# Attention and two expert layers on one core: a new order for the attention round, and another queue for the first k

## Chip, cores and metric

One core of a Trainium2 chip. The metric is the device time in microseconds of one execution. The kernel before takes 916.21 us, the median of three runs (915.29 to 916.43).

## What is computed

Attention over 4 batches, 8 heads, 576 positions, head size 64, all in float32, mixed with a linear memory by a gate per head; then two dense layers. The two layers are not touched by the change.

```python
scores = scale * np.matmul(q, k.transpose(0, 1, 3, 2))      # causal mask follows
a = np.exp(scores - scores.max(-1, keepdims=True)); a /= a.sum(-1, keepdims=True) + 1e-09
local = np.matmul(a, v)
q_p = phi(q)                                                # phi(x) = max(x, 0) + min(exp(x), 1)
mem_out = einsum('bhsd,bhde->bhse', q_p, M_prev) / (einsum('bhsd,bhd->bhs', q_p, z_prev)[..., None] + 1e-06)
g = 1.0 / (1.0 + np.exp(-beta))[None, :, None, None]
attn = g * mem_out + (1 - g) * local
# then: x = _moe_ref(attn, w_in, w_out, g_ln); out = _moe2_ref(x, w_gate, w_val, w_out)
```

## The kernel before

Attention works on pairs of heads: 16 pairs (4 batches by 4 pairs of heads). The 576 positions of a head are four blocks of 128 and a tail of 64; the tails of both heads of a pair are one block more (block 4). What is done for one pair is cut into 77 steps. The string `ORDER` (line 21) lists the steps of one round of a loop, each with a distance: in round `it`, the step `s2_p:0` works on pair `it`, `tk_p:1` on the next pair, `x0_c:-2` on the pair two before. `run` (line 506) walks through the list once per round, from round -3 on, and leaves out pairs that don't exist. The whole of attention stands under `tc.manual_schedule()`, so each engine's queue has its instructions in just this order, and an engine waits at the first one that isn't ready. What follows attention is ordered by the framework.

The steps, by engine (a number is that of a block of queries, or for `t`, `a` and `g` of keys):

- TensorE: `tq_p`, `tk_p`, `tf_p` transpose q, k and the memory's queries (L265); `s0_p` to `s4_p` are the scores (L352, three passes of float32r); `g0_p`, `g1_p`, `t0_p` to `t3_p`, `tt_p`, `tc_p` transpose the weights (L398 to L432); the sums over keys are `x0_m`, `x1_m` (the memory's part, L444) and `a00`, `a01`, `a10` to `a14` (L459), which write the two halves of a PSUM tile's partitions, one head each. `x0_m`, `a01` and `a00` make the first 256 queries, `x1_m` and `a14` to `a10` the other 320.
- VectorE: `s*_m` adds the mask and takes maxima (L372); `n01_r`, `n23_r`, `n4_r` turn sums into factors (L384, L385); `ph_m` is the memory's phi (L306, L307); `tq_l`, `tk_l` the low parts of q and k (L284, L295); `ph_r` the memory's norm (L321 to L323); copies `g1_c`, `tc_c`, `x0_c`; and, for the layer that follows, a piece of its weights a round: `cv_a` (L108, L109), `cv_b` (L117, L122), `cv_l` (L504).
- ScalarE: the exponentials `s*_e` (L380) and `ph_e`, the high parts `tq_h`, `tk_h`, the other copies out of PSUM, and `cv_r`, `cv_h`.
- GpSimd: `n*_p` scales the weights (L389), `ph_g` and `ph_s` are the memory's products (L311, L328), `cv_p` (L496).
- SyncE issues the loads `lq`, `lk`, `lv`, `lz`, `cv_d`.

PSUM: the scores and the three transposes of a pair take turns on two tiles (tag `s`), the transposed weights on two (`t`), the sums on two (`x`). A step that takes a tile waits until the step that reads its last content is done. The tile `ex` of the weights' conversion is there once: `cv_a` of one piece overwrites what `cv_l` of the piece before has read.

In the order of before the sums of a pair stand in two places: `x0_m x1_m a13 a12 a11 a14 a10 a01` in one round, and `a00` after the scores `s3_p` in the next.

Of the kernel before, what the change touches and what calls it, by code (L numbers as in the profile page):

```python
# [18 lines left out]


ORDER = """
n23_r:-1 s1_e:0 s4_m:0 tt_c:-1 tc_c:-1 s3_m:0 lk:1 cv_r:-1 n3_p:-1 s0_e:0 s4_e:0 x1_c:-2 a00:-2 g1_p:-1 tf_p:0
t3_p:-1 g1_c:-1 tf_c:0 n2_p:-1 t3_c:-1 x0_c:-2 s2_p:0 t2_p:-1 t0_p:-1 cv_b:-1 ph_e:1 t2_c:-1 n4_r:0 n01_r:0 tq_p:1
cv_p:-1 n1_p:0 lz:1 t0_c:-1 t1_p:-1 g0_p:-1 cv_h:-1 tq_h:1 s2_m:0 t1_c:-1 ph_m:1 tk_p:1 tk_h:1 x0_m:-1 x1_m:-1
a13:-1 tq_l:1 tk_l:1 ph_g:1 n0_p:0 n4_p:0 cv_d:1 lv:0 a12:-1 a11:-1 a14:-1 a10:-1 ph_r:1 lq:2 ph_s:1 s3_e:0 s2_e:0
a01:-1 s1_p:1 s0_p:1 s1_m:1 tt_p:0 s0_m:1 g0_c:-1 tc_p:0 s4_p:1 cv_l:-1 s3_p:1 cv_a:0
""".split()


# [21 lines left out]
def kernel(  # L51
# [16 lines left out]
    nc = tc.nc  # L68
# [82 lines left out]
    class Attention:  # L151
# [69 lines left out]
            return self.ps.tile(shape, F32, tag=tag, name=name, bufs=2)  # L221


        def load_qk(self, n, t, src):
            b, hp = pairs[n]
            for hh in range(2):
                nc.sync.dma_start(
                    t[:, : 8 * D].rearrange("p (c h d) -> p c h d", h=2, d=D)[:, :, hh],
                    src[b, 2 * hp + hh, :S0, :].rearrange("(c p) d -> p c d", p=P),
                )  # L230
            nc.sync.dma_start(
                t[0:64, 8 * D : 10 * D].rearrange("p (h d) -> p h d", h=2),
                src[b, 2 * hp : 2 * hp + 2, S0:, :].rearrange("h p d -> p h d"),
            )
# [2 lines left out]
            self.load_qk(n, self.qt[n % 2], q)  # L237

        def lk(self, n, r):
            self.load_qk(n, self.kt[n % 2], k)  # L240

        def lv(self, n, r):
            b, hp = pairs[n]
# [608 lines left out]
```

## Time and profile before

| what | us |
|---|---|
| median of three runs | 916.21 |
| the profiled execution | 914.82 |
| its span, first to last instruction | 913.0 |
| TensorE busy in the span | 888.3 |
| one round of attention in its steady part | 13.29 |

The profile is of one execution. Its page gives busy shares over the whole span, in which attention is the first quarter; answers for a stretch of time show one round. A line of a timeline has the start, the duration, engine, line, operation, what is written and read, shapes, and in brackets how long the engine was idle before and what released it. Matmul durations are modelled at their ends, so the time that a matmul group takes is read from its start to the next one's.

### The profile page before, as it was taken

To read this page: it belongs to the slowest core of one execution; us is meant where nothing else is said; L and a number is where in the kernel's file an instruction comes from. 1 tells how busy PE (TensorE), PEld (TensorE's weight loads), DVE (VectorE), ACT (ScalarE), POOL (GpSimd) and SP (SyncE) were. 2 spreads that over 40 slices of the span, in tenths; PEclk is the share of its full clock that TensorE was granted. 3 is DMA by queue.
4 is the path that set the end of the run, shared out by engine and by line. 5 is a ranking of instruction groups with operands and counts; after the bars stand their busy time and mean duration, and the time that the engine had idled before them with its cause. 6 is when DMAs were issued, how large, how long until landed. Compare 5 with 4: busy or idle time off the path is not lost.

```text
span 913.0 us, 13960 instructions
## 1 busy us (share of the span) xinstructions
PE 888.3 (97%) x5224; PEld 753.2 (82%) x5224; DVE 567.2 (62%) x1321; ACT 432.1 (47%) x941; POOL 267.0 (29%) x322
## 2 busy tenths in 40 slices
PE   5899999999989999999999999999999999999998
PEld 4788788787778998999998888888888888888887
DVE  5899999999587655664825158366349735232324
ACT  3799999998577455464535333112122212111111
POOL 4566665666565211112400034021014103000000
PEclk9899999999999999999999999999999999999999
DMA  5243533443122100110300013012003200000113
GB/s 127 51 94 81 115 90 89 97 104 88 47 70 71 47 24 24 36 58 24 116 1 1 1 53 109 23 27 67 1 1 106 79 0 1 1 1 1 47 46 116
DMA packets 76291, 48.62 MB, mean 53 GB/s; under 512 B 62656, under 2 KB 62656, under 8 KB 76224
## 3 DMA queue, kind: packets, MB, share of 16 engines
q1 hardware_dynamic: 76224, 47.74, 19.1%
q8 instruction: 41, 0.67, 0.3%
q14 instruction: 26, 0.21, 0.1%
HBM read 43.00 MB, written 4.72 MB: 52 GB/s over the span
## 4 chain that ended last, share of the span: by engine, by line
PE 87%; DVE 7%; POOL 2%; ACT 1%; issue 1%; DMA 1%; SPq 1%; DVEq 0%; POOLq 0%; ACTq 0%
PE gv L730 32%; PE po L749 16%; PE po L648 9%; PE sc L352 8%; PE h L597 7%; PE x L459 5%; PE x L444 2%; PE pl L636 1%; PE trq L265 1%; DVE p L372 1%; PE trk L265 1%; PE trf L265 1%; DVE exwo L109 1%; DVE exwo L108 0%; DVE exwo L119 0%
## 5 line engine op out<-in xcount | busy, mean ns | idle before, releaser
L736 DVE TENSOR_TENSOR sg<-sg,gv 128x512 f32<-128x512 f32 (+1 forms) x60 | 38.0, 633 | 176.5 <-ACT sg L735 176.5
L735 ACT ACTIVATE sg<-gv 128x512 f32<-128x512 f32 (+1 forms) x60 | 33.1, 552 | 233.7 <-PE gv L730 233.7
L730 PE MATMUL gv<-xx,gh 128*128 128x512 f32 (+1 forms) x480 | 136.2, 368 | 0.2 <-ACT xx L138 0.2
L730 PE MATMUL gv<-xx,vh 128*128 128x512 f32 (+1 forms) x480 | 136.1, 368 | 0.0
L648 PE MATMUL po<-lnT,woh 128*128 128x256 f32 x576 | 104.9, 284 | 1.1 <-ACT woh L575 0.7
L730 PEld LDWEIGHTS gv<-xx,gh 128*128 128x128 f32 x480 | 87.4, 189 | 16.1 <-issue 0.4
L730 PEld LDWEIGHTS gv<-xx,vh 128*128 128x128 f32 x480 | 87.1, 189 | 15.0
L648 PEld LDWEIGHTS po<-lnT,woh 128*128 128x128 f32 x576 | 90.5, 192 | 2.7 <-ACT woh L575 0.9
L389 POOL TENSOR_SCALAR p<-p,rs 128x256 f32<-128x256 f32 (+2 forms) x144 | 78.3, 561 | 36.4 <-ACT ex L112 16.4
L380 ACT ACTIVATE p<-p,nm 128x256 f32<-128x256 f32 (+2 forms) x144 | 82.7, 579 | 12.6 <-DVE nm L372 12.6
L730 PE MATMUL gv<-xx,vl 128*128 128x512 f32 (+1 forms) x240 | 88.4, 368 | 0.0
L730 PE MATMUL gv<-xx,gl 128*128 128x512 f32 (+1 forms) x240 | 88.3, 368 | 0.0
L352 PE MATMUL sc<-kh,q 128*128 128x256 f32 (+4 forms) x320 | 79.5, 340 | 9.0 <-DVE nm L372 5.4
L597 PE MATMUL h<-wih,xs 128*128 128x512 f32 x288 | 81.5, 396 | 2.9 <-DVE e L610 2.9
L749 PE MATMUL po<-oh,GVxs 128*128 128x512 f32 x216 | 84.2, 390 | 0.0
L749 PE MATMUL po<-ol,GVxs 128*128 128x512 f32 x216 | 84.2, 390 | 0.0
L749 PE MATMUL po<-oh,GVe 128*128 128x512 f32 x216 | 84.1, 389 | 0.0
L648 PE MATMUL po<-lnT,wol 128*128 128x256 f32 x288 | 81.5, 284 | 1.1 <-POOL wol L145 1.1
L756 DVE TENSOR_TENSOR X<-X,po 128x512 f32<-128x512 f32 x90 | 61.3, 683 | 22.7 <-PE po L749 22.7
L352 PEld LDWEIGHTS sc<-kh,q 128*128 128x128 f32 x320 | 54.2, 200 | 14.6 <-DVE nm L372 6.5
L597 PEld LDWEIGHTS h<-wih,xs 128*128 128x128 f32 x288 | 53.2, 189 | 14.0 <-ACT e L619 2.9
L372 DVE CUSTOM_DVE_ANT_0 p<-sc,mask 128x256 f32<-128x256 f32 (+3 forms) x128 | 55.9, 483 | 9.9 <-PE sc L352 9.9
(351 smaller groups left out, 1785.0 us busy)
## 6 DMA issues: line engine op xcount, KB each, us to landing
rawg<-in_moe_w_gate_dram SPq DMA_DIRECT2D x12, 512.0 KB, 3.9
rawv<-in_moe_w_val_dram SPq DMA_DIRECT2D x12, 512.0 KB, 3.9
rawo<-in_moe_w_out_dram SPq DMA_DIRECT2D x12, 512.0 KB, 3.5
out_dram<-X SPq DMA_DIRECT2D x18, 256.0 KB, 2.0
qt<-in_q_dram SPq DMA_DIRECT2D x32, 128.0 KB, 2.7
kt<-in_k_dram SPq DMA_DIRECT2D x32, 128.0 KB, 2.8
raw<-in_moe_w_in_dram SPq DMA_DIRECT2D x16, 256.0 KB, 3.4
vt<-in_v_dram SPq DMA_DIRECT2D x32, 128.0 KB, 3.6
```

Source lines behind the costliest of these rows:

```text
L352: nc.tensor.matmul(x, qs[c], kk[:, ks], start=m == 0, stop=m == 2)
L372: nc.vector.tensor_tensor_reduce(p, x, m, -1.0, 3.0e38, ALU.add, ALU.min, nm)
L380: nc.scalar.activation(p, p, AF.Exp, bias=nm, scale=-1.0, accum_out=r["sum"][:, c : c + 1])
L389: nc.gpsimd.tensor_scalar(p, p, r["rs"][:, c : c + 1], 1.0, ALU.mult, ALU.mult)
L459: nc.tensor.matmul(r["x", g][64 * hh : 64 * hh + 64, c0 : c0 + src.shape[1]], r["vt"][:, c : c + D], src, start=False, stop=j == 0,)
L597: nc.tensor.matmul(ph[:, j * 512 : j * 512 + 512], xs[:, s, c], w[:, j * 512 : j * 512 + 512], start=(c == 0 and s == 0 and w is hi), stop ...
L648: nc.tensor.matmul(po[:, :GW], w[:, m * P : m * P + P], L[:, x, c], start=(c == 0 and n == 0), stop=(c == NF1 - 1 and n == 2),)
L730: nc.tensor.matmul(ps[:, j, :w], wt[:, c, fs], xx[:, x, c], start=(c == 0 and n == 0), stop=(c == NC - 1 and n == 2),)
L735: nc.scalar.activation(sg[:, :w], ps[:, 0, :w], AF.Sigmoid)
L736: nc.vector.tensor_mul(sg[:, :w], sg[:, :w], ps[:, 1, :w])
L749: nc.tensor.matmul(po, GV[x][:, f, sl], wt[:, f], start=(f == 0 and n == 0), stop=(f == NCH - 1 and n == 2),)
L756: nc.vector.tensor_add(acc[:, t], acc[:, t], po)
```

## The change

The list `ORDER` is written anew: the same 77 steps, in another order and some with other distances. All sums of a pair are now one block at the head of a round, `x0_m a01 a00 x1_m a14 a13 a12 a11 a10`, of the pair two before. All five scores of a pair stand in the round with its own number (0), in the order 0, 1, 2, 4, 3; before, four of the five stood one round ahead. `lk` moves to distance 2. Where VectorE's queue read `ph_m tq_l tk_l ph_r s1_m s0_m cv_l cv_a n23_r s4_m tc_c s3_m g1_c x0_c cv_b n4_r n01_r s2_m` it now reads `n23_r s0_m x0_c s1_m tc_c s2_m s4_m g1_c cv_b n4_r n01_r s3_m ph_m cv_l cv_a tq_l tk_l ph_r`. GpSimd's `n3_p n2_p cv_p n1_p ph_g n0_p n4_p ph_s` (before, from its place in the round) becomes `ph_s n3_p n2_p cv_p n1_p ph_g n4_p n0_p`. The load of the first k is issued from ScalarE's queue.

```diff
 ORDER = """
-n23_r:-1 s1_e:0 s4_m:0 tt_c:-1 tc_c:-1 s3_m:0 lk:1 cv_r:-1 n3_p:-1 s0_e:0 s4_e:0 x1_c:-2 a00:-2 g1_p:-1 tf_p:0
-t3_p:-1 g1_c:-1 tf_c:0 n2_p:-1 t3_c:-1 x0_c:-2 s2_p:0 t2_p:-1 t0_p:-1 cv_b:-1 ph_e:1 t2_c:-1 n4_r:0 n01_r:0 tq_p:1
-cv_p:-1 n1_p:0 lz:1 t0_c:-1 t1_p:-1 g0_p:-1 cv_h:-1 tq_h:1 s2_m:0 t1_c:-1 ph_m:1 tk_p:1 tk_h:1 x0_m:-1 x1_m:-1
-a13:-1 tq_l:1 tk_l:1 ph_g:1 n0_p:0 n4_p:0 cv_d:1 lv:0 a12:-1 a11:-1 a14:-1 a10:-1 ph_r:1 lq:2 ph_s:1 s3_e:0 s2_e:0
-a01:-1 s1_p:1 s0_p:1 s1_m:1 tt_p:0 s0_m:1 g0_c:-1 tc_p:0 s4_p:1 cv_l:-1 s3_p:1 cv_a:0
+x0_m:-2 a01:-2 a00:-2 x1_m:-2 a14:-2 a13:-2 a12:-2 a11:-2 a10:-2 tt_p:-1 s0_p:0 n23_r:-1 cv_r:-1 s0_m:0 s1_p:0
+tc_p:-1 x0_c:-2 s1_m:0 tc_c:-1 x1_c:-2 tt_c:-1 ph_s:0 s2_p:0 s2_m:0 s4_p:0 g1_p:-1 s4_m:0 g0_p:-1 s0_e:0 tf_p:0
+s3_p:0 n3_p:-1 g1_c:-1 s1_e:0 n2_p:-1 g0_c:-1 s4_e:0 tf_c:0 t3_p:-1 cv_b:-1 t1_p:-1 ph_e:1 t3_c:-1 n4_r:0 tq_p:1
+t0_p:-1 n01_r:0 lz:1 cv_d:1 t1_c:-1 cv_p:-1 n1_p:0 s3_m:0 ph_m:1 cv_h:-1 cv_l:-1 cv_a:0 t2_p:-1 tk_p:1 tq_h:1
+t0_c:-1 tq_l:1 lv:0 lq:2 tk_h:1 tk_l:1 ph_g:1 t2_c:-1 lk:2 s2_e:0 n4_p:0 n0_p:0 ph_r:1 s3_e:0
 """.split()
-        def load_qk(self, n, t, src):
+        def load_qk(self, n, t, src, dma=nc.sync.dma_start):
             b, hp = pairs[n]
             for hh in range(2):
-                nc.sync.dma_start(
+                dma(
...
         def lk(self, n, r):
-            self.load_qk(n, self.kt[n % 2], k)
+            self.load_qk(n, self.kt[n % 2], k, nc.sync.dma_start if n else nc.scalar.dma_start)
```

## Rows read from the trace of the kernel before

**Rows 1.** The page: busy time (us, share of the span, instructions), and one costly group.
```profile
PE 888.3 (97%) x5224; PEld 753.2 (82%) x5224; DVE 567.2 (62%) x1321; ACT 432.1 (47%) x941; POOL 267.0 (29%) x322
...
L389 POOL TENSOR_SCALAR p<-p,rs 128x256 f32<-128x256 f32 (+2 forms) x144 | 78.3, 561 | 36.4 <-ACT ex L112 16.4
```

**Rows 2.** Busy time by stretch: length, busy us by engine (instructions), clock, DMA.
```profile
122.72:136.01 13.29, 13.29 (x109) 10.80 (x107) 12.42 (x42) 12.49 (x37) 8.39 (x13) 1.00 0.31 72
...
202.45:216.43 13.98, 13.69 (x109) 10.84 (x107) 13.29 (x42) 12.89 (x37) 9.59 (x14) 1.00 0.39 87
```

**Rows 3.** Timeline of TensorE in that round: start, duration, line, what, count.
```profile
125.53 0.63 PE L352 MATMUL sc<-kh,q 128*128 128x512 f32 x2
...
126.23 0.63 PE L352 MATMUL sc<-kh,q 128*128 128x512 f32 x2
...
127.01 0.65 PE L459 MATMUL x<-A,vt 128*64 128x256 f32 x4
...
135.15 0.71 PE L459 MATMUL x<-Bt,vt 128*64 128x320 f32 x4
135.69 0.39 PE L459 MATMUL x<-A,vt 128*64 128x128 f32 x4
136.01 0.50 PE L352 MATMUL sc<-kh,q 128*128 128x256 f32 x2
```

**Rows 4.** VectorE in that round: its waits (us in all, times, longest), then timeline.
```profile
DVE p L372 <- PE sc L352: 0.6, 2, 0.4
...
124.85 0.42 DVE L504 TENSOR_TENSOR wil<-ex,wih 128x256 fp32r<-128x256 f32 x1
125.30 0.29 DVE L108 TENSOR_SCALAR ex<-raw 128x256 int32<-128x256 int32 x1
...
129.69 0.15 DVE L384 SCALAR_TENSOR_TENSOR rs<-sum,o 128x1 f32<-128x1 f32 x1
...
129.95 0.64 DVE L384 SCALAR_TENSOR_TENSOR rs<-sum,o 128x4 f32<-128x4 f32 x1
...
132.32 0.83 DVE L307 SCALAR_TENSOR_TENSOR E<-qt,E 128x640 f32<-128x640 f32 x1
```

**Rows 5.** Timeline of GpSimd in that round.
```profile
126.26 2.48 POOL L389 TENSOR_SCALAR p<-p,rs 128x512 f32<-128x512 f32 x4 [1.49 <-ACT ex L112]
129.85 0.73 POOL L496 TENSOR_TENSOR ex<-ex 128x256 f32<-128x256 f32 x1 [1.11 <-DVE rs L384]
...
133.23 1.55 POOL L311 TENSOR_TENSOR G<-E,zm 128x640 f32<-128x640 f32 x1 [1.29 <-DVE E L307]
```

**Rows 6.** Timelines of VectorE and GpSimd near 204.5 us.
```profile
204.57 1.44 DVE L504 TENSOR_TENSOR wil<-ex,wih 128x256 fp32r<-128x256 f32 x1
...
204.44 1.28 POOL L590 TENSOR_TENSOR xs<-X,xs 128x512 fp32r<-128x512 f32 x1
```

**Rows 7.** Timelines of VectorE and GpSimd near 226.5 us.
```profile
226.14 0.51 DVE L504 TENSOR_TENSOR wil<-ex,wih 128x256 fp32r<-128x256 f32 x1
...
226.68 0.35 DVE L108 TENSOR_SCALAR ex<-raw 128x256 int32<-128x256 int32 x1
...
226.95 0.28 DVE L109 TENSOR_SCALAR ex<-raw 128x256 int32<-128x256 int32 x1
...
226.35 1.04 POOL L389 TENSOR_SCALAR p<-p,rs 128x128 f32<-128x128 f32 x2
```

**Rows 8.** Timelines of VectorE and GpSimd in later stages, at 687 and 617 us.
```profile
687.88 0.67 DVE L119 SCALAR_TENSOR_TENSOR exv<-rawv,exv 128x512 f32<-128x512 uint16 x1
...
687.51 1.53 POOL L142 TENSOR_SCALAR vh<-exv 128x512 fp32r<-128x512 f32 x1 [5.38 <-DVE exv L698]
...
617.92 1.51 DVE L109 TENSOR_SCALAR exg<-rawg 128x512 int32<-128x512 int32 x1
...
617.80 1.34 POOL L145 TENSOR_TENSOR ol<-exo,oh 128x512 fp32r<-128x512 f32 x1
```

**Rows 9.** Timeline of TensorE at the start: the first scores.
```profile
9.44 0.77 PE L352 MATMUL sc<-kh,q 128*128 128x256 f32 x2 [1.64 <-DVE q L284]
```

More of the change, by code (lines that the diff above doesn't have):

```diff
@@ L230, in load_qk @@
                 )
-            nc.sync.dma_start(
+            dma(
                 t[0:64, 8 * D : 10 * D].rearrange("p (h d) -> p h d", h=2),
```

## Prediction

> **What bounds the kernel now.** I read the page's busy shares first: TensorE is busy in 888.3 of 913.0 us, VectorE in 62% [rows 1]. These are averages over three stages, and the change touches only the first, attention, so I cut out one round of it, from the first score matmul of one pair to that of the next [rows 2] (the first row). There TensorE is busy in all 13.29 us at a granted clock of 1.00, and VectorE in 12.42, GpSimd in only 8.39. So TensorE sets the pace of a round, and VectorE is next with very little in hand. How little shows in VectorE's waits and its order of time [rows 4]: in a round it waits for TensorE twice, 0.6 us in all, the longer time 0.4. One more stretch is not work: L384 for the sums of blocks 0 and 1 lasts 0.64 us, while the same kind of instruction just before it takes 0.15. It began 0.10 us into GpSimd's L496 and ended with it [rows 5]. So 0.49 us of a round VectorE stands behind a GpSimd instruction. That leaves 13.29 - 0.6 - 0.49 = 12.2 us of its own work and gaps.
>
> The price of such a stand is in the trace once more, larger. At 204.57 VectorE's L504 took 1.44 us instead of 0.42, because GpSimd's L590 had begun 0.13 earlier [rows 4, 6]. That round lasted 13.98 us instead of 13.29 [rows 2]: a hold of 1.02 us on VectorE cost 0.69 of TensorE's time. This is the row on which I rest most.
>
> **TensorE's order.** The sums over keys now stand in two blocks a round; they become one. Each border costs a little [rows 3]. Six score matmuls of 512 columns: the first three take 0.70 us to the next start, the last three, ahead of a sum, 0.78: 0.08 to enter. A sum of 4x320 columns takes 0.54, so 4x128 should take 0.22; ahead of scores it takes 0.32: 0.10 to leave. The borders from transposes into the sums and from the sums to transposes stay, once each. New is one more turn from transposes to scores and back; no row prices it alone (a round has two already), and its bounds are 0 and the 0.10 of the dearer border removed. I take 0. So TensorE needs 0.18 us less (bounds 0.08 and 0.18): a round of about 13.1, if nothing else comes late.
>
> **VectorE's order is what I expect to decide.** In the new list the queue of VectorE reads: scores' maxima of 0, 1, 2 and 4, then cv_b, n4_r, n01_r, the maxima of 3, ph_m, cv_l, cv_a, tq_l, tk_l, ph_r. GpSimd's reads ph_s, n3, n2, cv_p, n1, ph_g, n4, n0. Two neighbours matter. n4_r and n01_r still stand right behind cv_b, whose end starts cv_p, so the stand of 0.49 us stays. And cv_l and cv_a now follow ph_m directly, and the end of ph_m starts ph_g, GpSimd's longest instruction of a round. In the order of before cv_l and cv_a run from 124.85 to 125.7, while GpSimd is idle (1.49 us up to 126.26) [rows 5], and take 0.42 and, the first half of cv_a, 0.29 [rows 4].
>
> Step by step from the end of L307, the last of ph_m, called T: L311 starts at T + 0.08 (133.15 to 133.23) [rows 4, 5]. L504 of cv_l has started by then, and ends near T + 0.34. L108 needs its own engine's L504 to be done (it overwrites what L504 reads) and starts 0.03 behind it, near T + 0.38. By then L311 has waited for 0.3 us. Who goes first is shown by a place with the same three [rows 7]: L504 from 226.14 to 226.65 and L108 at 226.68, while GpSimd had an instruction to begin from 226.35; that one lasted about half its pair's 1.04 and L108 took 0.35 instead of 0.29, so GpSimd went between the two. I take the same here. Then L311 lasts to about T + 1.73 (0.08 + 1.55 + 0.10 of waiting). In rows 6 the held instruction lost 0.13 less than what was left of GpSimd's at its start (1.28 - 0.13 = 1.15 left, 1.02 lost). So L108 loses 1.73 - 0.38 - 0.13 = 1.22 us, each round. Bounds: 0, if L108 goes first; 1.22 and another 0.56, if the second half of cv_a, L109, then falls behind n4, too, 0.56 being the mean of that group of GpSimd [rows 1].
>
> The Trainium skill (SBUF — State Buffer, Terms) says that VectorE and GpSimd arbitrate for one pair of ports, held exclusively for a full instruction, the loser blocking fully; GPSIMD Engine Reference (Key points) limits it to VectorE's instructions in a two-port mode or with two SBUF inputs. By that the trace's 1.44 and 0.64 agree. The rule doesn't say who goes next, and speaks against any cv_a placed behind ph_m; by it alone each of cv_a's two instructions may lose, which is the second rival.
>
> VectorE's new round: 12.2 own + 0.49 behind cv_p + 1.22 behind ph_g = 13.9, more than TensorE's 13.1, so VectorE sets the pace. Its waits for TensorE don't vanish wholly: in rows 2 and 6 a hold of 1.02 cost 0.69, where 1.02 - 0.6 = 0.42 would be left if all waiting had been used up, so 0.27 stayed. Bounds 0 and 0.6; I take 0.27, the measured one. 14.18 us, 0.89 more than now. cv_l of the pair before, cv_a and ph_g of the next pair meet in rounds 1 to 14 of the 16: 14 x 0.89 = 12.5 us.
>
> **The rest.** Queues of SyncE: lk moves from one to two pairs ahead, behind cv_d, lv and lq; it still has a whole round until its transposes, and takes nothing. The first k goes out from ScalarE's queue, three issues, beside the first q. ScalarE has nothing to do before q lands. But the first scores wait for VectorE's q (low part), not for k: 1.64 us [rows 9]. So k earlier gains nothing, and the cover is q's own chain; if both loads share engines and q lands later, it costs what q loses. Beginning and end of the stage: the order of the first pair changes, the last block comes a part of a round later. The trace prices neither. The nearest rows are the wait of 1.64 [rows 9], which might vanish, and one stand of 1.22 carried through to the end. I take 0, bounds -1.6 and +1.2. The two later stages run the same instructions; their start moves with attention's end. ScalarE loses nothing: it has the same work.
>
> **Sum.** The profiled execution took 914.8 us around its span of 913.0, 1.4 under the median 916.2. 914.8 + 12.5 = 927.3; on the median 928.7. I say 928.
>
> **Rivals.** First, VectorE keeps its turn through cv_l and cv_a, and ph_g waits. For it: at 687.51 GpSimd began L142, and VectorE's L119, which came 0.37 later, still took its turn first: 0.67 us, while L142 lasted 1.53 [rows 8]. Against it: L119 is of another kind, and L108 stands 0.03 behind L504 [rows 4, 7]. Then TensorE's 13.1 holds: 15 x -0.18 = -2.7, or 913.5 by the median (-1.2 with the dearer border, 915).
> Second, both halves of cv_a are held. For it: L109 at 617.92 took 1.51, GpSimd's L145 having begun 0.12 earlier [rows 8]. Against it: at 226.95 L109 took 0.28, though GpSimd's next began at about 226.86 [rows 7]; and as here behind an L108 that had waited. 14 x 0.56 = 7.8 more: 936.
> Third, the hold is there but shorter (ph_g later, so that L108 is through and only L109 meets it, or more slack than I count): a hold of 0.5 to 0.8 eats the slack and TensorE's 0.18 and leaves 914 to 919.
>
> **Chances.** Forecast 0.40, second rival 0.25, first 0.23, third 0.12. A difference of 0.2% (1.8 us) is about what can be told here: below 914.4 faster, above 918.0 slower. Of the first rival 0.17 falls under faster and 0.06 under same; of the third 0.06 same and 0.06 slower; all else slower. The range goes from 913 to 938: it leaves out 0.1 below (the first rival with a shorter start) and 0.1 above (both held and the waits at their upper bound).
>
> **What would show it.** Right: in a round of the new profile L108 takes about 1.5 us and ends just behind L311; a round lasts 14.2; TensorE waits for VectorE's q and maxima, about 1 us a round. Wrong: L108 at 0.29 with L311 over 2 us (first rival), L109 over 0.8 (second), a round of 13.1 with TensorE busy throughout.

## The result and the profile of the changed kernel

The changed kernel takes 927.56 us, the median of four runs (926.57 to 928.03); beside it the kernel before took 915.75 (915.09 to 916.43, four runs). The ratio is 1.0131, 95% interval 1.0116 to 1.0146: slower by 11.8 us, or 1.3%. The profiled execution took 928.03 around a span of 926.2.

In the changed file every line behind 240 stands one further on: L311 of `ph_g` is L312, L504 of `cv_l` is L505, L384 is L385. L108 and L109 of `cv_a` keep their numbers. `ORDER` has 74 steps in both kernels, not the 77 said above. "Held" and "a stand" mean below that an instruction of VectorE lasts longer than elsewhere because GpSimd has its turn.

The page of the changed kernel, busy time by engine (us, share of the span, instructions), beside [rows 1]:

```profile
PE 892.2 (96%) x5224; PEld 758.3 (82%) x5224; DVE 585.6 (63%) x1321; ACT 432.6 (47%) x941; POOL 267.2 (29%) x322
```

The same instructions, and VectorE is busy 18.4 us longer. One round in its steady part, from one pair's transposes of k to the next pair's, as in [rows 2] (length, busy us of PE, PEld, DVE, ACT, POOL, granted clock, DMA):

```profile
122.98:137.08 14.10, 13.52 (x108) 11.00 (x107) 13.52 (x42) 12.51 (x35) 8.69 (x12) 1.00 0.37 87
```

14.10 us instead of 13.29, at the same granted clock of 1.00. TensorE now has 0.58 us without work, and VectorE's 42 instructions are busy 1.10 longer. The timelines of VectorE and GpSimd in that round (start, us, engine, line, operation, what it works on) beside [rows 4, 5]:

```profile
123.41 0.83 DVE L308 SCALAR_TENSOR_TENSOR E<-qt,E 128x640 f32<-128x640 f32 x1
124.15 0.42 DVE L505 TENSOR_TENSOR wil<-ex,wih 128x256 fp32r<-128x256 f32 x1
124.60 1.55 DVE L108 TENSOR_SCALAR ex<-raw 128x256 int32<-128x256 int32 x1
126.05 0.31 DVE L109 TENSOR_SCALAR ex<-raw 128x256 int32<-128x256 int32 x1
...
134.69 0.73 DVE L385 SCALAR_TENSOR_TENSOR rs<-sum,o 128x1 f32<-128x1 f32 x1
...
124.32 1.66 POOL L312 TENSOR_TENSOR G<-E,zm 128x640 f32<-128x640 f32 x1 [1.44 <-DVE E L308]
...
134.66 0.74 POOL L497 TENSOR_TENSOR ex<-ex 128x256 f32<-128x256 f32 x1 [0.93 <-DVE ex L122]
```

L108 takes 1.55 us where it took 0.29: the row of L312 begins at 124.32, while L505 still runs; L108 begins 0.28 later and ends 0.17 behind L312. That is 1.26 us a round. The second stand is the old one, behind `cv_p` (L497): it now meets `n4_r` (0.73 for 0.15). The waits of TensorE and VectorE over seven rounds, 100 to 200 us (us in all, times, longest):

```profile
PE sc L353 <- DVE kl L296: 2.5, 8, 0.4
PE sc L353 <- DVE nm L373: 2.0, 7, 0.3
...
DVE p L373 <- PE sc L353: 1.3, 7, 0.2
```

TensorE waits for VectorE about twice a round, where [rows 2] shows it busy throughout; VectorE's waiting fell from 0.6 to 0.2 a round.

Over the whole execution, by the starts of the same work on TensorE in both profiles:

| from | to | before | after | difference |
|---|---|---|---|---|
| start of the span | first pair's transposes of k | 6.50 | 6.08 | -0.4 |
| those | second pair's | 18.14 | 16.94 | -1.2 |
| those | sixteenth pair's (14 rounds) | 187.75 | 199.70 | +11.95 |
| those | first `h` of the next layer | 25.99 | 26.57 | +0.6 |
| that | first `gv` of the last layer | 216.05 | 218.33 | +2.3 |
| that | end of the span | 458.6 | 458.6 | 0 |

Attention's rounds carry nearly all of it. The middle layer, which the change doesn't touch, lost 2.3. TensorE's timeline there, before and then after (in brackets the idle time ahead and its releaser), and then a window by engine for each (length, PE busy, granted clock, DMA):

```profile
257.49 1.03 PE L597 MATMUL h<-wih,xs 128*128 128x512 f32 x2 [2.47 <-DVE e L610]
```
```profile
268.24 1.75 PE L637 MATMUL pl<-ident,e 128*128 128x128 f32 x8 [2.31 <-ACT e L620]
286.57 1.11 PE L637 MATMUL pl<-ident,e 128*128 128x128 f32 x4 [3.80 <-DVE lnT L139]
```
```profile
280.00:290.00 10.00, 7.90 (x55) 1.00 0.33 107
```
```profile
286.00:290.00 4.00, 3.43 (x16) 0.50 0.06 4
290.00:294.00 4.00, 4.00 (x27) 0.70 0.40 129
```

The framework orders that layer, and it laid the first sums and transposes otherwise than before: TensorE now stands 3.80 us ahead of one group of transposes, and the granted clock, which falls within that stand, is 0.50 until about 292.4 (the 0.70 is the mean over a window with both levels), the lower of its two levels (1.2 of 2.4 GHz). In the whole layer TensorE is idle for 6.4 us instead of 5.4. Profiles of experiments below part the two. Experiments 1, 5, 6 and 7 have this order of TensorE's instructions there, too, with 6.3 to 6.5 idle. In 1 and 7 this stretch of the lower clock lasts 3.4 us, and the layer takes 217.09 in each; in 5, 6 and the changed kernel it lasts 6.8, and the layer takes 218.2 to 218.3. (The kernel before has one stretch at the lower clock in that layer, of 3.4.) So of the 2.3 lost, 1.0 goes with the order and what comes with it, and 1.2 with the longer stretch at the lower clock. Why the framework chose this order was not tried.

### The profile page after: what moved, and what is told of

Same layout as the page of the kernel before. It is cut to its first block, busy times and chain, and to the rows that moved or that the text cites. A ratio compares the mean times of both kernels' runs of the same rounds, so it can differ in the third digit from the quotient of the medians.

```text
span 926.2 us, 13965 instructions
## 1 busy us (share of the span) xinstructions
PE 892.2 (96%) x5224; PEld 758.3 (82%) x5224; DVE 585.6 (63%) x1321; ACT 432.6 (47%) x941; POOL 267.2 (29%) x322
## 4 chain that ended last, share of the span: by engine, by line
PE 73%; DVE 17%; issue 5%; ACT 2%; POOL 2%; DMA 1%; SPq 0%; DVEq 0%; ACTq 0%; POOLq 0%
PE gv L731 32%; PE po L750 16%; PE po L649 9%; PE h L598 7%; PE sc L353 4%; DVE q L285 2%; DVE p L373 2%; PE pl L637 1%; DVE E L308 1%; DVE rs L385 1%; DVE kl L296 1%; DVE nr L322 1%; ACT A L135 1%; DVE rs L386 1%; DVE E L307 1%
## 5 line engine op out<-in xcount | busy, mean ns | idle before, releaser
L649 PE MATMUL po<-lnT,woh 128*128 128x256 f32 x576 | 107.1, 288 | 0.3 <-ACT X L653 0.3
L381 ACT ACTIVATE p<-p,nm 128x128 f32<-128x128 f32 (+2 forms) x144 | 83.2, 585 | 17.3 <-DVE nm L373 17.3
L353 PE MATMUL sc<-kh,q 128*128 128x128 f32 (+4 forms) x320 | 82.3, 345 | 8.9 <-DVE nm L373 5.3
L390 POOL TENSOR_SCALAR p<-p,rs 128x256 f32<-128x256 f32 (+2 forms) x144 | 80.8, 579 | 16.4 <-DVE rs L386 15.5
L142 POOL TENSOR_SCALAR gh<-exg 128x512 fp32r<-128x512 f32 x12 | 8.9, 750 | 183.0 <-PE gv L731 142.1
```

Of the source, the lines that this page charges most:

```text
L353: nc.tensor.matmul(x, qs[c], kk[:, ks], start=m == 0, stop=m == 2)
L381: nc.scalar.activation(p, p, AF.Exp, bias=nm, scale=-1.0, accum_out=r["sum"][:, c : c + 1])
L390: nc.gpsimd.tensor_scalar(p, p, r["rs"][:, c : c + 1], 1.0, ALU.mult, ALU.mult)
L649: nc.tensor.matmul(po[:, :GW], w[:, m * P : m * P + P], L[:, x, c], start=(c == 0 and n == 0), stop=(c == NF1 - 1 and n == 2),)
```

## The experiments

The theory: VectorE sets the round, because `cv_a` falls behind `ph_g`. The rivals: TensorE's new order itself is slower, the k load is, or the hold has another cause than the one I gave.

**1. `cv_h`, `cv_l`, `cv_a` ahead of `ph_m`.** Undoes the one neighbourhood that the theory blames.

```diff
-t0_p:-1 n01_r:0 lz:1 cv_d:1 t1_c:-1 cv_p:-1 n1_p:0 s3_m:0 ph_m:1 cv_h:-1 cv_l:-1 cv_a:0 t2_p:-1 tk_p:1 tq_h:1
+t0_p:-1 n01_r:0 lz:1 cv_d:1 t1_c:-1 cv_p:-1 n1_p:0 s3_m:0 cv_h:-1 cv_l:-1 cv_a:0 ph_m:1 t2_p:-1 tk_p:1 tq_h:1
```

> The new kernel with one thing moved: cv_h, cv_l and cv_a stand ahead of ph_m instead of behind it, so that on VectorE they run between the maxima of block 3 and ph_m, when GpSimd has finished n1 and waits for ph_m. Theory (the hold of L108 behind ph_g makes the whole loss): L108 takes 0.29 us, VectorE's round is 12.2 + 0.49 + 0.27 = 13.0, TensorE's 13.1 sets the pace; 15 rounds at 1.0 less than 14.12 give 927.6 - 15.3 = 912. Rival (the new order of scores and PSUM tiles is itself the slow thing, the hold only fills its slack): rounds stay at 13.9 to 14.1, 925 to 928.

911.14 us (910.72 to 912.15), 0.9961 of before, interval 0.9945 to 0.9976. Timelines of its VectorE and GpSimd in a round, then the busy times of a round (columns as above):

```profile
128.83 0.42 DVE L505 TENSOR_TENSOR wil<-ex,wih 128x256 fp32r<-128x256 f32 x1
129.28 0.29 DVE L108 TENSOR_SCALAR ex<-raw 128x256 int32<-128x256 int32 x1
129.49 0.29 DVE L109 TENSOR_SCALAR ex<-raw 128x256 int32<-128x256 int32 x1
...
131.12 1.55 POOL L312 TENSOR_TENSOR G<-E,zm 128x640 f32<-128x640 f32 x1 [2.31 <-DVE E L308]
```
```profile
115.98:129.03 13.05, 13.05 (x109) 10.88 (x108) 12.42 (x42) 12.29 (x35) 8.37 (x12) 1.00 0.39 95
```

The hold is gone, TensorE is busy in the whole round, and the round is 13.05: 0.24 below before. Three steps moved by a place are worth 16.4 us (15.6 when each kernel is set against the runs of before beside it), more than the whole loss. So TensorE's new order is a gain, and the place of `cv_l` and `cv_a` is the loss.

**2. The same neighbourhood in the order of before:** `cv_l` and `cv_a` taken from the end of the list and put behind `ph_m`, nothing else.

```diff
-cv_p:-1 n1_p:0 lz:1 t0_c:-1 t1_p:-1 g0_p:-1 cv_h:-1 tq_h:1 s2_m:0 t1_c:-1 ph_m:1 tk_p:1 tk_h:1 x0_m:-1 x1_m:-1
+cv_p:-1 n1_p:0 lz:1 t0_c:-1 t1_p:-1 g0_p:-1 cv_h:-1 tq_h:1 s2_m:0 t1_c:-1 ph_m:1 cv_l:-1 cv_a:0 tk_p:1 tk_h:1 x0_m:-1 x1_m:-1
...
-a01:-1 s1_p:1 s0_p:1 s1_m:1 tt_p:0 s0_m:1 g0_c:-1 tc_p:0 s4_p:1 cv_l:-1 s3_p:1 cv_a:0
+a01:-1 s1_p:1 s0_p:1 s1_m:1 tt_p:0 s0_m:1 g0_c:-1 tc_p:0 s4_p:1 s3_p:1
```

> The kernel before, with cv_l and cv_a moved right behind ph_m, everything else as it was. Theory: L108 is held 1.22 us behind ph_g in each round here, too; by the sum a round of 14.2, by the price of the one hold in the trace of before (0.69 for 1.02) 14.1; 15 rounds at 0.7 to 0.9 more: 926 to 929. Rival (the hold is only dear in the new order): 916 to 919.

935.67 us (934.24 to 936.38), ratio 1.0224 (1.0209 to 1.0239). L108 takes 1.52 in a round. It costs more than expected, since the move uncovers a second stand: with `cv_l` and `cv_a` gone from their old place, `n23_r` comes while `ph_s` runs (GpSimd's row below the three of VectorE):

```profile
128.54 0.65 DVE L384 SCALAR_TENSOR_TENSOR rs<-sum,o 128x4 f32<-128x4 f32 x1
132.11 1.52 DVE L108 TENSOR_SCALAR ex<-raw 128x256 int32<-128x256 int32 x1
138.28 0.48 DVE L384 SCALAR_TENSOR_TENSOR rs<-sum,o 128x4 f32<-128x4 f32 x1
...
137.49 1.26 POOL L328 TENSOR_TENSOR E<-E,nr 128x640 f32<-128x640 f32 x1 [2.43 <-DVE nr L323]
```

Three holds a round instead of one. The round is about 14.8 instead of 13.29, and TensorE waits 0.8 for the low part of q in each. The mechanism repeats in the old order; its price alone can't be read here.

**3. The first k from ScalarE's queue, in the kernel before.** Of the change only `load_qk` and this line of `lk`:

```diff
-            self.load_qk(n, self.kt[n % 2], k)
+            self.load_qk(n, self.kt[n % 2], k, nc.sync.dma_start if n else nc.scalar.dma_start)
```

> The kernel before with the first k's load issued from ScalarE's queue, nothing else. In the new kernel q landed at 4.98 us instead of 4.00 and the first scores began at 10.86 instead of 9.44. Theory (both loads share the engines and q, which the chain waits for, lands about 1 us later): first scores about 1.4 us later, and the whole 0.6 to 1.4 more: 916.4 to 917.2. Rival (the later start comes from the new order of the first round, or is made up later): 915.8, no change.

914.6 us (914.23 to 915.67), ratio 0.9997 (0.9988 to 1.0005): no difference. The first scores start 1.45 us later than in [rows 9] (10.89), q landing later, and the next rounds make it good: the sixteenth pair's transposes come 0.3 earlier than before.

**4. The reverse:** experiment 1 with the first k from SyncE's queue.

```diff
-            self.load_qk(n, self.kt[n % 2], k, nc.sync.dma_start if n else nc.scalar.dma_start)
+            self.load_qk(n, self.kt[n % 2], k, nc.sync.dma_start)
```

> The order with cv_h, cv_l and cv_a ahead of ph_m, and the first k issued from SyncE's queue again, as in the kernel before. In the old order ScalarE's queue for the first k put the first scores off from 9.44 to 10.89 us, and the rounds after that made it good, since VectorE and not the load set them. Theory: here too the first round is made good, no difference from the 911.1 us that this order has with ScalarE's queue, within 0.8. Rival: in the new order TensorE sets the pace from the first full round on, nothing is made good, and the 1.4 us at the start come through: 909.7.

910.33 us (909.72 to 911.52), ratio 0.9945 (0.9931 to 0.9958). Its interval overlaps that of experiment 1, so the queue can't be told to matter. In its profile q lands at 3.99 instead of 4.95 and the first scores start at 10.36 instead of 10.73, but the sixteenth pair's transposes come at 208.30 instead of 207.90: nothing of the earlier start comes through. It has the best median of all versions here.

**5. `ph_g` in two instructions** of 256 and 384 columns, in the changed kernel.

```diff
-            nc.gpsimd.tensor_mul(
...
+            G, E = (r[x].rearrange("p (c x) -> p c x", x=P) for x in "GE")
+            for c0, c1 in ((0, 2), (2, 5)):
+                nc.gpsimd.tensor_mul(
+                    G[:, c0:c1], E[:, c0:c1], r["z"].unsqueeze(1).to_broadcast([P, c1 - c0, P])
+                )
```

> The new kernel with ph_g issued as two GpSimd instructions, of 256 and of 384 columns instead of one of 640; the result is the same. Theory (the hold lasts as long as one GpSimd instruction): L108 is let through after the first piece, about 0.7 us long, and loses about 0.4 instead of 1.22; if L109 also gets its turn ahead of the second piece, a round is 13.3 and the time 927.6 - 14 x 0.8 = 916; if L109 falls behind the second piece, it loses about 0.9 in its place and the time is 925 to 928. Rival (the hold comes from waiting for ph_g's result or something else, not instruction by instruction): L108 stays at 1.5 and the time at 928.

927.4 us (926.95 to 927.98), as slow as the changed kernel. Timelines of VectorE and GpSimd (L314 is `ph_g`):

```profile
138.38 0.71 DVE L108 TENSOR_SCALAR ex<-raw 128x256 int32<-128x256 int32 x1
139.01 1.09 DVE L109 TENSOR_SCALAR ex<-raw 128x256 int32<-128x256 int32 x1
...
138.10 1.86 POOL L314 TENSOR_TENSOR G<-E,zm 128x256 f32<-128x256 f32 x2 [1.44 <-DVE E L308]
```

L108 loses 0.42 and L109 0.80: together 1.22, where L108 alone lost 1.26. L108 gets its turn behind the first piece, and L109 waits for the second: the turn goes by single instructions, and the cut only shares the loss out.

**6. `cv_p` left out** of the changed kernel.

```diff
-t0_p:-1 n01_r:0 lz:1 cv_d:1 t1_c:-1 cv_p:-1 n1_p:0 s3_m:0 ph_m:1 cv_h:-1 cv_l:-1 cv_a:0 t2_p:-1 tk_p:1 tq_h:1
+t0_p:-1 n01_r:0 lz:1 cv_d:1 t1_c:-1 n1_p:0 s3_m:0 ph_m:1 cv_h:-1 cv_l:-1 cv_a:0 t2_p:-1 tk_p:1 tq_h:1
```

> The changed kernel with cv_p left out, so the weights of the next layer lack their exponents; nothing else is touched. cv_p is the GpSimd instruction behind which n4_r stands: 0.73 us instead of 0.15, 0.58 us of VectorE's round. Theory (VectorE sets the round, and every hold is a term of its sum): the round falls from 14.12 to about 13.55, 14 rounds, 8 us less: 919.5. If the whole of L108's hold is still there, its duration stays 1.5. Rival (the round is set by a chain through the low parts of q and k and the scores, on which n4_r has no place): no change, 927.5.

921.46 us (921.09 to 922.34), 6.1 below the changed kernel. The stand of `n4_r` is gone and L108's is unchanged (VectorE's timeline, then the busy times of a round):

```profile
131.68 0.16 DVE L385 SCALAR_TENSOR_TENSOR rs<-sum,o 128x1 f32<-128x1 f32 x1
135.26 1.53 DVE L108 TENSOR_SCALAR ex<-raw 128x256 int32<-128x256 int32 x1
```
```profile
120.00:133.67 13.67, 13.38 (x109) 11.01 (x108) 13.07 (x42) 12.51 (x35) 7.89 (x11) 1.00 0.38 91
```

The round falls by 0.43 for 0.57 taken from VectorE: this hold, too, counts while VectorE sets the pace, here at about three quarters. The rival, a round set by the low parts alone, falls.

**7. Two buffers for `ex`** in the changed kernel, so that L108 needn't wait for the end of L505. My reason for the hold was the gap of 0.03 between the two.

```diff
-            r["ex"] = self.sb.tile([P, 2, 256], I32, tag="ex", name=f"ex{n}")
+            r["ex"] = self.sb.tile([P, 2, 256], I32, tag="ex", name=f"ex{n}", bufs=2)
```

> The changed kernel with two buffers for the tile ex, so that L108 of cv_a overwrites nothing that L505 of cv_l reads, and needn't wait for its end; all steps stand where they stood. In the changed kernel L108 starts 0.03 us behind the end of L505, and instructions of VectorE that don't depend on each other start some 0.08 ahead of the end of the one before. Theory A (the gap lets GpSimd in): L108 takes 0.3 us and GpSimd's L312 waits; either L109 is through as well, L312 lasts about 2 us and the time is 911 to 913, or L109 is held in its place for about 1 us and the time stays at 924 to 927. Theory B (an instruction with one input lets GpSimd in wherever it stands): L108 is held for 1.3 to 1.5 us as it is now, 926 to 928.

927.77 us (927.39 to 927.88). L108 now starts 0.08 ahead of the end of L505, without a gap, and is held for longer:

```profile
125.25 0.42 DVE L505 TENSOR_TENSOR wil<-ex,wih 128x256 fp32r<-128x256 f32 x1
125.59 1.66 DVE L108 TENSOR_SCALAR ex<-raw 128x256 int32<-128x256 int32 x1
...
125.42 1.66 POOL L312 TENSOR_TENSOR G<-E,zm 128x640 f32<-128x640 f32 x1 [1.44 <-DVE E L308]
```

The gap is not what lets GpSimd in.

**8. Another kind of instruction behind `cv_l`:** in the changed kernel `cv_b` takes the place of `cv_a`, which goes ahead of `ph_m`.

```diff
-s3_p:0 n3_p:-1 g1_c:-1 s1_e:0 n2_p:-1 g0_c:-1 s4_e:0 tf_c:0 t3_p:-1 cv_b:-1 t1_p:-1 ph_e:1 t3_c:-1 n4_r:0 tq_p:1
-t0_p:-1 n01_r:0 lz:1 cv_d:1 t1_c:-1 cv_p:-1 n1_p:0 s3_m:0 ph_m:1 cv_h:-1 cv_l:-1 cv_a:0 t2_p:-1 tk_p:1 tq_h:1
+s3_p:0 n3_p:-1 g1_c:-1 s1_e:0 n2_p:-1 g0_c:-1 s4_e:0 tf_c:0 t3_p:-1 t1_p:-1 ph_e:1 t3_c:-1 n4_r:0 tq_p:1
+t0_p:-1 n01_r:0 lz:1 cv_d:1 t1_c:-1 cv_p:-2 n1_p:0 s3_m:0 cv_a:0 ph_m:1 cv_h:-2 cv_l:-2 cv_b:-1 t2_p:-1 tk_p:1 tq_h:1
...
+            r["raw"] = self.sb.tile([P, 256, 2], I32, tag="raw", name=f"raw{n}", bufs=3)
...
+            r["ex"] = self.sb.tile([P, 2, 256], I32, tag="ex", name=f"ex{n}", bufs=3)
```

> What is held behind ph_m: is it whatever VectorE starts after GpSimd has asked, or only an instruction with one input? The changed kernel, with cv_b (L117, L122, two inputs each) in the place behind cv_l where cv_a stood, and cv_a ahead of ph_m; so that this is possible, ex and raw have three buffers and a piece of weights takes one round longer (cv_p, cv_h, cv_l at distance 2). In the changed kernel L312 asks 0.91 us behind the start of L308, while L505 runs, and goes ahead of L108. Theory A (whoever asks first is next, whatever its kind): L117 takes 1.6 to 1.7 us instead of 0.41, L312 1.66, the hold on VectorE's round is as large as now. Theory B (two inputs back to back keep their turn, as L119 did in the rows at 687 us): L117 and L122 take 0.42 each, L312 lasts 2.2 to 2.6, nothing on VectorE is held there, and a round is 13.1 to 13.4. The time under A, with the hold of n4_r behind cv_p gone or in another place, 920 to 928; under B 909 to 916.

Timelines of VectorE and GpSimd:

```profile
125.59 0.42 DVE L505 TENSOR_TENSOR wil<-ex,wih 128x256 fp32r<-128x256 f32 x1
125.92 1.77 DVE L117 SCALAR_TENSOR_TENSOR ex<-raw,ex 128x256 int32<-128x256 int32 x1
127.62 0.42 DVE L122 SCALAR_TENSOR_TENSOR ex<-raw,ex 128x256 f32<-128x256 uint16 x1
...
136.42 0.16 DVE L385 SCALAR_TENSOR_TENSOR rs<-sum,o 128x1 f32<-128x1 f32 x1 [0.79 <-ACT p L381]
...
125.75 1.66 POOL L312 TENSOR_TENSOR G<-E,zm 128x640 f32<-128x640 f32 x1 [1.99 <-DVE E L308]
127.40 1.87 POOL L390 TENSOR_SCALAR p<-p,rs 128x576 f32<-128x576 f32 x3
```

L117, with two inputs, is held for 1.36. So theory A of this run holds: L312 asked while L505 ran, and whatever VectorE brought next waited. The time, 935.84 (935.25 to 936.24), missed both ranges. A round is 14.35 instead of 14.12, as `n4_r`, no longer covered by `cv_b`, waits 0.79 for ScalarE's sum. And the middle layer takes 222.98 instead of 218.33: TensorE has yet another order there and is idle for 11.3 us instead of 6.4. That this comes from weights ready a round later is likely and not shown. One thing stays open: at 127.40 GpSimd's next, L390, was ready before L122 came, and L122 wasn't held.

**9. The border of the sums alone.** First attempt, on experiment 1: `a00` taken out of the head of the list, put behind `s3_p:0`, and its copy `x0_c` ahead of `cv_b`.

```diff
-x0_m:-2 a01:-2 a00:-2 x1_m:-2 a14:-2 a13:-2 a12:-2 a11:-2 a10:-2 tt_p:-1 s0_p:0 n23_r:-1 cv_r:-1 s0_m:0 s1_p:0
+x0_m:-2 a01:-2 x1_m:-2 a14:-2 a13:-2 a12:-2 a11:-2 a10:-2 tt_p:-1 s0_p:0 n23_r:-1 cv_r:-1 s0_m:0 s1_p:0
...
+s3_p:0 a00:-2 n3_p:-1 g1_c:-1 s1_e:0 n2_p:-1 g0_c:-1 s4_e:0 tf_c:0 t3_p:-1 x0_c:-2 cv_b:-1 t1_p:-1 ph_e:1 t3_c:-1 n4_r:0 tq_p:1
```

> The order with cv_h, cv_l and cv_a ahead of ph_m, in which TensorE never waits, with one step of the sums, a00, taken out of the block and put behind the scores of block 3 again (the copy of that half, x0_c, goes ahead of cv_b). This is the second border of the old order alone. By the prediction two turns cost 0.18 us a round: a round of 13.23 instead of 13.05, some 15 rounds, 2.7 us more, 913.8. Rival: the gaps at the borders are only a shift within the matmuls that follow, 0: 911.1.

938.74 us (936.65 to 939.24), rounds of 15.2. It tells nothing of the border: VectorE reaches `x0_c` before TensorE reaches `a00`, and waits (VectorE's timeline):

```profile
126.22 0.42 DVE L135 COPY X<-x 128x256 f32<-128x256 f32 x1 [2.03 <-PE x L460]
```

**10. The border once more**, with `a00` behind the scores of block 0, whose maxima cover the copy:

```diff
-x0_m:-2 a01:-2 a00:-2 x1_m:-2 a14:-2 a13:-2 a12:-2 a11:-2 a10:-2 tt_p:-1 s0_p:0 n23_r:-1 cv_r:-1 s0_m:0 s1_p:0
+x0_m:-2 a01:-2 x1_m:-2 a14:-2 a13:-2 a12:-2 a11:-2 a10:-2 tt_p:-1 s0_p:0 a00:-2 n23_r:-1 cv_r:-1 s0_m:0 s1_p:0
```

> Once more the border of the sums alone, in a place where no copy waits for it: the order with cv_h, cv_l and cv_a ahead of ph_m, with a00 taken out of the block and put between the scores of block 0 and those of block 1; its copy x0_c stays behind the maxima of block 0, which cover it (s0_m takes 0.5 us, the four matmuls about 0.4 with both borders). Putting a00 behind the scores of block 3, with its copy ahead of cv_b, made VectorE wait 2.03 us a round and told nothing of the border. By the prediction a round of 13.05 + 0.18 = 13.23, some 15 rounds: 2.7 us more than 911.1, 913.8. Rival: no price, 911.1.

918.7 us (918.05 to 920.23), 7.6 above experiment 1; a round is 13.75, 0.70 longer, not 0.18. Its timeline of TensorE, and the copy of ScalarE that feeds the sums; then the same of experiment 1:

```profile
122.26 0.39 PE L460 MATMUL x<-A,vt 128*64 128x128 f32 x4
122.48 0.71 PE L445 MATMUL x<-f,mt 128*64 128x320 f32 x4
...
123.13 2.47 PE L460 MATMUL x<-Bt,vt 128*64 128x192 f32 x16
...
126.55 0.28 PE L353 MATMUL sc<-kl,q 128*128 128x128 f32 x1
126.75 0.65 PE L460 MATMUL x<-A,vt 128*64 128x256 f32 x4
127.33 0.50 PE L353 MATMUL sc<-kh,q 128*128 128x256 f32 x2
...
123.11 0.60 ACT L135 COPY Bt<-t6b 128x512 f32<-128x512 f32 x1
```
```profile
130.15 0.82 PE L460 MATMUL x<-A,vt 128*64 128x128 f32 x8
130.80 0.71 PE L445 MATMUL x<-f,mt 128*64 128x320 f32 x4
...
131.45 2.11 PE L460 MATMUL x<-Bt,vt 128*64 128x192 f32 x16
...
134.49 0.28 PE L353 MATMUL sc<-kl,q 128*128 128x128 f32 x1
134.61 0.46 PE L353 MATMUL sc<-kh,q 128*128 128x256 f32 x2
...
130.99 0.61 ACT L135 COPY Bt<-t7b 128x512 f32<-128x512 f32 x1
```

Half of the 0.70 is a wait within the sums: the group of 16 takes 0.36 more, since without `a00` ahead of it it begins 0.58 before ScalarE's copy of `Bt` is done (123.71), and in experiment 1 only 0.15 before (131.60). No bracket shows that wait, as the row merges the 16; the profile's answer on the tile `Bt` does, with 0.5 in which the weight loads stand for that copy. Taken singly, the fifth of them, the first of `a12`, starts at 123.76, 0.05 behind the end of that copy and 0.46 after the fourth; in experiment 1 it starts 0.16 after it, with the copy done. The other 0.34 is left for the border and what follows it. Of that, 0.08 can be read at the entry (0.20 to the next start for 0.12) and 0.15 at `a00` itself: 0.58 to the next start, where in the block it adds 0.43 (0.65 with it, 0.22 without). So a border in that place costs 0.23 as read, more than the 0.18 of the prediction, and 0.34 at most. And a step taken out of a block also takes away the cover of the one behind it.

## Why the prediction was right

**VectorE's order decides: right, and so was its size.** L108's stand was put at 1.22 and measured 1.26 (1.55 for 0.29) in a steady round; L109 was free, as said. A round was put at 14.18 and is 14.1. VectorE's sum was 12.2 + 0.49 + 1.22 + 0.27 of waiting; measured, the stand behind `cv_p` is 0.58, that behind `ph_g` 1.26 and the waiting 0.2. The price of a hold in [rows 6] was the right row to rest on.

**The reason given for it was partly wrong.** I read [rows 7] as GpSimd going in because L108 stands 0.03 behind L504. That row had little to carry it: L108 lost 0.06 there, and 1.26 here, so that the step came out right is in part luck. Experiment 7 shows that the gap doesn't matter at this place, and experiment 8 that an instruction with two inputs fares no better. What the runs share is that `ph_g` is ready while an instruction of VectorE runs, and the next one of `cv_a` or `cv_b` waits for it. The first rival fell, but the argument that I set against it (L119 is of another kind) is not what decides here; why L119 kept its turn in [rows 8] stays open, with the L122 of experiment 8. The Trainium skill (SBUF — State Buffer, SBUF: two separate sides) says that where the two meet at the port pair they share, the one that starts first gets the pair for its whole instruction. The stands of 1.26, 1.36 and 1.37 agree with this when being ready first is taken as the start, and L122 does not.

**The second and third rival.** L109 is held in one round of the changed kernel, the first, and in experiment 5. That first round has no `cv_l` yet, so L108 ran when L312 got ready, and L109 came next (timelines of VectorE and GpSimd):

```profile
24.15 0.28 DVE L108 TENSOR_SCALAR ex<-raw 128x256 int32<-128x256 int32 x1
24.36 1.65 DVE L109 TENSOR_SCALAR ex<-raw 128x256 int32<-128x256 int32 x1
...
24.32 1.54 POOL L312 TENSOR_TENSOR G<-E,zm 128x640 f32<-128x640 f32 x1 [1.73 <-DVE E L308]
```

L109 lost 1.36 there. So what waits is the next instruction in the queue, whichever half of `cv_a` it is. The prediction counted rounds 1 to 14 alone, so this stand was missed. The third rival had this case of L109 alone, but a shorter hold, which did not come.

**TensorE's gain of 0.18: right in sign, too small.** Without the hold the round is 13.05, 0.24 below before, and 13.1 was forecast. Experiment 10 prices one border at 0.23 as read, 0.34 at most. The residual of 0.27 taken for the waits was in turn a little high (0.2).

**TensorE's waits: about half of what was said.** I expected about 1 us a round, for q and the maxima. It is 0.58, for the low part of k and the maxima, and not for q.

**Start, end and later stages: 0 was wrong three times, and it cancelled.** The start gained 1.6, which is the lower bound that I had kept; the end of the stage lost 0.6; the middle layer lost 2.3, which had no bound at all, as I took the same instructions for the same time (1.0 went with their order, 1.2 with the clock). The fourteen rounds gave 11.95 where 12.5 was forecast. The sum of the profiled executions is +13.2; that of before lay 0.9 below its own median beside it and that of the changed kernel 0.5 above, so the medians differ by 11.8. That the 928 came out to half a microsecond is luck, with three terms off by 1.6, 0.6 and 2.3. What stood on rows, the fourteen rounds, was off by 0.55.

**The load of k: nothing, as said,** in the old order (experiment 3); in the new one (experiment 4) no difference can be told. And q does land later for it (4.98 instead of 4.00), the risk that I had named.

## What to carry to other kernels

When an order is rewritten for one engine, write down for each other engine the new neighbours, above all the VectorE instructions that follow the one whose end starts a long GpSimd instruction: the next of them can stand for nearly GpSimd's whole duration, once a round. A step that can run just ahead of that trigger instead of just behind it costs nothing there; here three names moved by one place were worth about 16 us. And before a step is taken out of its place, look for what it covered: in experiments 2, 8, 9 and 10 a wait came out that had been hidden, and in 9 it was ten times what was to be measured.

## What the hardware showed that I had not expected

- VectorE's L108, which reads every second word of an int32 tile and has one input, is held as fully by GpSimd's instruction as one with two inputs: it lost 1.26 beside L312's 1.66, where L117 lost 1.36.
- A long GpSimd instruction in two pieces doesn't save the two of VectorE behind it anything to speak of: 0.42 + 0.80 = 1.22, for 1.26.
- VectorE without a gap is held for more, not less (1.37 for 1.26): it comes 0.11 earlier and waits for the same end.
- What reads PSUM showed no stand. Between 45 and 240 us of the twelve profiles, the copy of `x0_c` began 110 times with 0.2 us or more of a GpSimd `TENSOR_TENSOR` still to run, and took 0.42 to 0.43, as it did the 29 times that GpSimd was idle (0.41 to 0.43). The short instruction of `tq_l` (64 columns) did so 78 times and took 0.22, as it did 66 times with GpSimd idle. So `tq_l`, put right behind `ph_m` instead of `cv_l` and `cv_a`, might cost nothing there; that was not run.
